# Delta rule and two mixers on one core: chunks of 64 on 64x64 array tiles, inverses by substitution on VectorE

## The chip, the cores and the metric

The kernel runs on one core of a Trainium2 chip. The metric is the device time of one execution in microseconds (us); lower is better. Engines are named as in the profile: PE (TensorE, matrix products), PEld (PE's weight loads, which run beside its products), DVE (VectorE), ACT (ScalarE), POOL (GpSimd), and SP, whose queue issues all DMAs here.

## What is computed

Four batches, eight heads, 768 tokens and 48 columns a head; everything is fp32. First the delta rule, a recurrence over the tokens, then a low-rank token mixer and a channel mixer (weights of 384x1536 and 1536x384):

```python
for t in range(S):                                  # attention, each head by itself
    y[t] = q[t] @ state
    state = state + beta[t] * outer(k_n[t], v[t] - k_n[t] @ state)
x  = y of the 8 heads side by side                  # (4, 768, 384)
u  = x + (x.T @ U @ V).T                            # rank 32
out = u + relu(u @ w_ch1) @ w_ch2
```

Here k_n is k divided by its norm.

## The kernel before

Tokens are taken in chunks of 128. In a chunk, with G[t, s] = k_t.k_s beta_s for s < t and S0 the state before it, the unknowns w solve (I + G) w = v - k S0; then y and the new state are products with w. So a chunk has a part that needs no state (`transposes`, `inverse`) and a part that does (`recur`).

`inverse` (line 319) runs for half of the heads (4) at a time. It makes the Gram products (`p_g`, L334, on 48 rows of the array, the two heads of a pair on the upper and the lower half of its rows), masks them into `bt`, `mt` and `qk` (L343), and builds the inverses of 32x32 blocks on PE: three rounds of `p_x` (L356) with two DVE operations each (L360, L361), then three levels of `p_m` and `p_x` (both through `per_head`, L250), each with a DVE transpose (L258), an expansion to block-diagonal form on POOL (`w_d`, L266), a mask (L370) and a subtraction (L375). A last level, `p_z` and `p_v`, makes 64x64 blocks. In all those products a 128x128 stationary matrix, mostly zeros, meets a moving one of 32 or 128 columns.

`recur` (L394) does `p_b` (L407), `rhs` on DVE, `p_c`, a copy `w` on ACT, `p_r`, a copy, `p_w` (these two with 64x64 stationary matrices, all in one corner of the array), the state (`p_s`, L438) and `p_y` (L454, L463). `mixer` (L475) is a batch's `p_tt`, then twice: `p_h`, `p_u`, 36 products `p_f` (L507) and 36 `p_o` (L521) of 384 columns. Each fp32 product is two matmul instructions with a weight load each in the profile; a transpose is one.

The order of the program is set by a heap of (time, step): each part's steps get a start and a distance. The mixer of a batch is spread over the next batch's chunks, and the last mixer has nothing beside it. The compiler's scheduler orders each engine's instructions from there. `load_weights` turns 27 slices of float64 weights into fp32, with seven DVE operations and one on POOL each, in the first 395 us.

Of the kernel before, what the change touches and what calls it, by code (L numbers as in the profile page):

```python
# [25 lines left out]
def kernel(  # L26
# [24 lines left out]
    NCH = S // C  # L51
# [20 lines left out]
    def ps_att(shape, name):  # L72
        return psum.tile(shape, FP32, name=name, tag="att", bufs=4)

    def ps_gram(shape, name):
        return psum.tile(shape, FP32, name=name, tag="gram", bufs=2)
# [5 lines left out]
    ident = const.tile([128, 128], FP32, name="ident")  # L82
    make_identity(nc, ident)

    def block_ones(t, m):
        nc.gpsimd.memset(t, 1.0)
        tv = t.rearrange("p (a i) -> p a i", i=m)
        n = C // m
        nc.gpsimd.affine_select(
            out=tv, in_=tv, pattern=[[-m, n], [0, m]], base=0,  # L90
            channel_multiplier=1, compare_op=ALU.is_ge, fill=0.0,
        )
        nc.gpsimd.affine_select(
            out=tv, in_=tv, pattern=[[m, n], [0, m]], base=m - 1,
            channel_multiplier=-1, compare_op=ALU.is_ge, fill=0.0,
        )

    def keep_upper(t):
        nc.gpsimd.affine_select(
            out=t, in_=t, pattern=[[1, C]], base=0,  # L100
            channel_multiplier=-1, compare_op=ALU.is_gt, fill=0.0,
        )

    def compact(name, t):
        c_t = const.tile([128, BK], FP32, name=name)
        nc.vector.tensor_reduce(
            out=c_t, in_=t.rearrange("p (a i) -> p i a", i=BK), axis=AX.X, op=ALU.add
        )
        return c_t

    bd = {m: const.tile([128, C], FP32, name=f"bd{m}") for m in (4, 8, 16, BK, HC)}
    for m, t in bd.items():
        block_ones(t, m)
    mask_u = const.tile([128, C], FP32, name="mask_u")
    nc.gpsimd.memset(mask_u, 1.0)
    keep_upper(mask_u)
    mask_b = const.tile([128, C], FP32, name="mask_b")
    nc.gpsimd.tensor_tensor(out=mask_b, in0=mask_u, in1=bd[BK], op=ALU.mult)
    mask_m = const.tile([128, C], FP32, name="mask_m")
    nc.gpsimd.tensor_tensor(out=mask_m, in0=mask_u, in1=mask_b, op=ALU.subtract)  # L120

    ident_c = compact("ident_c", ident)
    base_c = compact("base_c", bd[4])
    nc.vector.tensor_scalar_mul(base_c, base_c, -1.0)
    # lower off-diagonal blocks of m within the blocks of 2 m
    level_c = []
    for m in (4, 8, 16, BK):
        pool, tag = (conv, "power") if m < BK else (const, "mask_z")
        lev = pool.tile([128, C], FP32, name=f"lev{m}", tag=tag)
        nc.gpsimd.tensor_tensor(out=lev, in0=bd[2 * m], in1=bd[m], op=ALU.subtract)  # L130
        nc.gpsimd.affine_select(
            out=lev, in_=lev, pattern=[[-1, C]], base=0,
            channel_multiplier=1, compare_op=ALU.is_gt, fill=0.0,
        )
        if m < BK:
            level_c.append(compact(f"level{m}", lev))
    mask_z = lev

    def pads(name):
        ts = [const.tile([128, H, DP], FP32, name=f"{name}{i}") for i in range(2)]  # L140
        for t in ts:
            nc.vector.memset(t[:, :, D:DP], 0.0)
        return ts

    kpads, kbpads, qpads = pads("kpad"), pads("kbpad"), pads("qpad")
    # the states of two heads on the partitions, zero outside of a head's own columns
    states = [
        [const.tile([128, NP // 2, 2 * D], FP32, name=f"state{i}{g}") for g in range(2)]
        for i in range(2)
    ]  # L150
    for t in states[0] + states[1]:
        nc.vector.memset(t, 0.0)

    beta_sb = const.tile([BH, S], FP32, name="beta_sb")
    betas = const.tile([128, NCH, BH], FP32, name="betas")
    w1_sb = const.tile([128, KT, DFF], FP32, name="w1_sb")
    w2_sb = const.tile([128, FT, DM], FP32, name="w2_sb")
    u_sb = const.tile([128, NCH, R], FP32, name="u_sb")
    v_sb = const.tile([R, S], FP32, name="v_sb")

    def load_beta():
        nc.sync.dma_start(out=beta_sb, in_=beta.rearrange("b h s -> (b h) s"))
        p_bt = ps_att([128, NCH, BH], "p_bt")
        for c in range(NCH):
            nc.tensor.transpose(
                p_bt[:, c], beta_sb[:, c * C : (c + 1) * C], ident[0:BH, 0:BH]
            )
        nc.vector.tensor_copy(out=betas, in_=p_bt)
# [3 lines left out]
    def weight_slices():  # L172
        for t in range(KT):
            for f in range(0, DFF, WIDE):
                at = slice(f, f + WIDE)
                yield w1_sb[:, t, at], moe_w_ch1[t * 128 : (t + 1) * 128, at], None
        for f in range(FT):
            yield w2_sb[:, f], moe_w_ch2[f * 128 : (f + 1) * 128, :], None
        for s0 in range(0, S, WIDE):
            yield v_sb[:, s0 : s0 + WIDE], moe_V[:, s0 : s0 + WIDE], None  # L180
        yield u_sb.rearrange("p c r -> p (c r)"), moe_U, NCH

    def load_weights():
        """float64 to fp32. The upper word h has the sign, 11 bits of exponent and 20 of mantissa:
        with the exponent moved to fp32's bias they are an fp32 number, to which the lower word's
        part of the mantissa is added, which rounds. Below fp32's normal numbers, the exponent
        stops at 0."""
        for dst, src, groups in weight_slices():
# [10 lines left out]
            power_t = conv.tile([128, n], I32, name="power")  # L199
            upper_t = conv.tile([128, n], I32, name="upper")  # L200
# [31 lines left out]
    HH = H // 2  # L232
    PP = NP // 2
    raw, made, xs = {}, {}, {}

    def load(n):
        b, c = divmod(n, NCH)
        for name, src in (("k", k), ("q", q), ("v", v)):
            t = loads.tile([128, H, D], FP32, name=f"{name}_raw")
            nc.sync.dma_start(  # L240
                out=t, in_=src[b, :, c * C : (c + 1) * C, :].rearrange("h p d -> p h d")
            )
            raw[n, name] = t

    def over_heads(t):
        return t[:, None, :].to_broadcast([128, HH, BK])

    def per_head(ps, lhsT, rhs):
        for h in range(HH):
            nc.tensor.matmul(ps[:, h], lhsT[:, h], rhs[:, h], start=True, stop=True)  # L250

    def pair(t, j):
        return t[:, 2 * j : 2 * j + 2].rearrange("p h d -> p (h d)")

    def swapped(x):
        """Compact blocks, each transposed."""
        w_c = comp.tile([128, HH, BK], FP32, name="w_c")
        nc.vector.transpose(  # L258
            w_c.rearrange("p h i -> p (h i)"), x.rearrange("p h i -> p (h i)")
        )  # L260
        return w_c

    def expand(x, tag):
        """Compact blocks as a block-diagonal matrix for each head."""
        w_d = dense.tile([128, HH, C], FP32, name=tag)
# [10 lines left out]
    def transposes(n):  # L276
# [31 lines left out]
        for src, dst, copy in (  # L308
# [5 lines left out]
            for j in range(NP):  # L314
                nc.tensor.transpose(p_t[:, j], pair(src, j), ident)  # L315
# [279 lines left out]
```

## Time and profile before

| what | value |
|---|---|
| median of 3 runs | 1530.19 us (1515.23 to 1539.02) |
| profiled execution, first to last instruction (its span) | 1532.0 us |
| PE busy | 1485.9 us, 97% |
| DVE, POOL, ACT busy | 587.3, 363.7, 160.7 us |

The page gives the profiled execution no time beside its span; the span lies 1.8 us above the median, inside the runs' spread, so sums made against the span stand for the time. A matmul's duration in the profile reaches from its start to a modelled end and overlaps with the next one's, so the pace of a group is read from where it and the next group start.

### The profile page before, as it was taken

What the parts mean: (1) busy time and instruction counts of PE and PEld (TensorE: products, weight loads), DVE (VectorE), ACT (ScalarE), POOL (GpSimd) and SP (SyncE); (2) the same over time, 40 slices, a digit from 0 to 9 for tenths busy, and PEclk for the clock granted to TensorE, in tenths of its full rate; (3) what the DMA queues carried; (4) which work ended last, traced back from release to release, by engine and by line L of the source; (5) the groups of instructions that cost most, each with busy time, mean ns of one, the idle gap of its engine ahead of it and who ended that gap; (6) DMA issues with size and microseconds to landing.
All of it is one profiled execution on the core that took longest, in us unless ns stands there. A gap on an engine that the chain in (4) does not pass through costs nothing.

```text
span 1532.0 us, 20099 instructions
## 1 busy us (share of the span) xinstructions
PE 1485.9 (97%) x8238; PEld 1221.9 (80%) x8238; DVE 587.3 (38%) x1698; ACT 160.7 (10%) x386; POOL 363.7 (24%) x324
## 2 busy tenths in 40 slices
PE   6999899899999999999999999999999999999999
PEld 5999899899788887777877888787787888786555
DVE  5544665655524443343423442324423433321000
ACT  1000100100101111110111110101101000100110
POOL 3332242332222232132121231221231231120000
PEclk9855655655669998899677995799878997879889
DMA  3101111100100000000000010001000000000000
GB/s 90 42 22 37 47 36 42 47 26 22 26 1 16 22 21 6 16 21 12 16 11 6 22 27 0 16 1 26 22 1 6 11 11 6 1 1 16 0 16 16
DMA packets 82811, 30.10 MB, mean 20 GB/s; under 512 B 76480, under 2 KB 79552, under 8 KB 82720
## 3 DMA queue, kind: packets, MB, share of 16 engines
q1 hardware_dynamic: 82720, 28.81, 7.7%
q8 instruction: 66, 1.08, 0.3%
q14 instruction: 25, 0.20, 0.0%
HBM read 24.08 MB, written 4.72 MB: 19 GB/s over the span
## 4 chain that ended last, share of the span: by engine, by line
PE 92%; DVE 6%; issue 1%; POOL 1%; ACT 0%; DMA 0%; POOLq 0%; SPq 0%; DVEq 0%
PE p_f L507 16%; PE p_o L521 13%; PE p_m L250 12%; PE p_x L356 12%; PE p_x L250 11%; PE p_y L463 4%; PE p_g L334 3%; PE p_c L250 3%; PE p_w L250 3%; PE p_v L250 2%; PE p_r L250 2%; PE p_z L250 2%; PE p_s L438 2%; PE p_t L315 2%; PE p_y L454 2%; PE p_h L493 1%
## 5 line engine op out<-in xcount | busy, mean ns | idle before, releaser
L266 POOL TENSOR_TENSOR w_d<-w_c,bd 128x512 f32<-128x512 f32 x192 | 249.4, 1305 | 763.2 <-DVE w_c L258 750.5
L507 PE MATMUL p_f<-ut,w_sb 128*128 128x384 f32 x576 | 265.7, 604 | 2.8 <-ACT ut L501 2.8
L521 PE MATMUL p_o<-w_sb,h_f 128*128 128x384 f32 x576 | 207.9, 499 | 0.0
L250 PEld LDWEIGHTS p_m<-x_c,bt 128*128 128x128 f32 x1152 | 196.1, 256 | 14.0 <-issue 3.8
L250 PEld LDWEIGHTS p_x<-m_c,w_d 128*128 128x128 f32 x1152 | 192.3, 251 | 18.7 <-issue 9.9
L250 PE MATMUL p_m<-x_c,bt 128*128 128x32 f32 x1152 | 197.3, 329 | 0.7 <-DVE x_c L361 0.7
L250 PE MATMUL p_x<-m_c,w_d 128*128 128x32 f32 x1152 | 191.5, 324 | 0.0
L507 PEld LDWEIGHTS p_f<-ut,w_sb 128*128 128x128 f32 x576 | 123.2, 231 | 70.8 <-issue 30.4
L356 PEld LDWEIGHTS p_x<-x_c,bt 128*128 128x128 f32 x768 | 133.6, 260 | 20.6 <-issue 11.8
L521 PEld LDWEIGHTS p_o<-w_sb,h_f 128*128 128x128 f32 x576 | 103.5, 192 | 54.5 <-issue 1.2
L356 PE MATMUL p_x<-x_c,bt 128*128 128x32 f32 x768 | 135.4, 333 | 7.7 <-DVE x_c L361 7.7
L375 DVE TENSOR_TENSOR x_c<-x_c,p_x 128x128 f32<-128x128 f32 x144 | 41.5, 288 | 220.6 <-PE p_x L250 220.6
L360 DVE TENSOR_TENSOR x_c<-p_x,base_c 128x128 f32<-128x128 f32 x144 | 41.0, 290 | 214.7 <-PE p_x L356 214.7
L370 DVE TENSOR_TENSOR m_c<-p_m,level 128x128 f32<-128x128 f32 x144 | 42.0, 292 | 190.3 <-PE p_m L250 190.3
L266 POOL TENSOR_TENSOR w_d<-x_c,bd 128x512 f32<-128x512 f32 x48 | 61.0, 1278 | 93.9 <-DVE x_c L375 91.4
L515 ACT ACTIVATE h_f<-p_f 128x384 f32<-128x384 f32 x96 | 47.1, 491 | 342.4 <-PE p_f L507 342.4
L356 PEld LDWEIGHTS p_x<-ident_c,bt 128*128 128x128 f32 x384 | 58.6, 226 | 16.4 <-DVE bt L343 10.1
L356 PE MATMUL p_x<-ident_c,bt 128*128 128x32 f32 x384 | 63.1, 306 | 3.8 <-DVE bt L343 3.2
L334 PE MATMUL p_g<-kq,kbt 48*128 48x256 f32 x384 | 61.6, 434 | 4.5 <-DVE qk L343 3.3
L463 PE MATMUL p_y<-w,qk 128*128 128x48 f32 x384 | 65.0, 325 | 0.0
L531 DVE TENSOR_TENSOR o_sb<-p_o,x 128x384 f32<-128x384 f32 x24 | 13.3, 556 | 133.1 <-PE p_o L521 133.1
L250 PEld LDWEIGHTS p_z<-w_d,mt 128*128 128x128 f32 x384 | 57.1, 226 | 9.1 <-POOL w_d L266 5.3
(96 smaller groups left out, 1546.5 us busy)
## 6 DMA issues: line engine op xcount, KB each, us to landing
wide<-in_moe_w_ch_dram SPq DMA_DIRECT2D x24, 384.0 KB, 3.1
k_raw<-in_k_dram SPq DMA_DIRECT2D x24, 192.0 KB, 2.5
q_raw<-in_q_dram SPq DMA_DIRECT2D x24, 192.0 KB, 3.0
v_raw<-in_v_dram SPq DMA_DIRECT2D x24, 192.0 KB, 2.6
out_dram<-o_sb SPq DMA_DIRECT2D x24, 192.0 KB, 1.9
wide<-in_moe_V_dram SPq DMA_DIRECT2D x2, 96.0 KB, 2.0
wide<-in_moe_U_dram SPq DMA_DIRECT2D x1, 192.0 KB, 2.6
beta_sb<-in_beta_dram SPq DMA_DIRECT2D x1, 96.0 KB, 2.1
```

The source lines that it names most:

```text
L250: nc.tensor.matmul(ps[:, h], lhsT[:, h], rhs[:, h], start=True, stop=True)
L266: nc.gpsimd.tensor_tensor(out=w_d.rearrange("p h (a i) -> p h a i", i=BK), in0=x[:, :, None, :].to_broadcast([128, HH, NB, BK]), in1=bd[BK ...
L315: nc.tensor.transpose(p_t[:, j], pair(src, j), ident)
L334: nc.tensor.matmul(p_gs[par][:, i], kbt[lo : lo + D, j], kq[lo : lo + D, j], start=True, stop=True,)
L356: nc.tensor.matmul(p_x[:, h], bt[:, h], ident_c if it == 0 else x[:, h], start=True, stop=True)
L360: nc.vector.tensor_tensor(out=x, in0=p_x, in1=over_heads(base_c), op=ALU.mult)
L370: nc.vector.tensor_tensor(out=m_c, in0=p_m, in1=over_heads(mask), op=ALU.mult)
L375: nc.vector.tensor_tensor(out=x_new, in0=x, in1=p_x, op=ALU.subtract)
L463: nc.tensor.matmul(p_y[:, h], qk[:, h], w[:, h], start=(c == 0 and h == 0), stop=(h == HH - 1), skip_group_check=True,)
L507: nc.tensor.matmul(p_f, w1_sb[:, t, f * 128 : (f + 1) * 128], ut[:, t], start=(t == 0), stop=(t == KT - 1),)
L515: nc.scalar.activation(h_f, p_f, ACTF.Relu)
L521: nc.tensor.matmul(p_o, hs[f][:, c * C - g : (c + 1) * C - g], w2_sb[:, f], start=(f == 0), stop=(f == FT - 1),)
```

## The change

The chunk becomes 64 tokens (`L`), so there are 12 to a batch. A unit is half of a batch, 6 chunks of 8 heads; its work without state is done at once, and there are 8 units.

- The heads lie as 4 slots (pair j, parity par) times 2 halves g. Products of `grams`, `recur` (64x64 stationary matrices, 48 or 2x64 columns) and `below` (32x32) each use a quarter or less of the array; the order `QUADS` goes round its four quarters.
- The explicit inverse by doubling is gone, with its POOL expansions. A unit's 192 diagonal 32x32 blocks are brought to 96 partitions by row of blocks: `pg` is written to a DRAM scratch in pieces of 128 bytes (4 DMAs), read back as 96x1024 (1 DMA), inverted by 31 steps of two DVE operations each (`prod`, then a subtraction from `xt`), written to DRAM (1 DMA) and read back into `zt` and `zc` (6 DMAs). `below` makes the block under the diagonal with `p_x` and `p_v` (48 products each).
- `p_r` and `p_w` fall away; a chunk has five groups of 8 products, `p_b`, `p_y`, `p_c`, `p_s`, `p_y`.
- k, q and v come in 24 smaller DMAs a unit in place of 3 a chunk. PSUM has two tiles of two banks (`pair`) for `p_g`, `p_x`, `p_v`, `p_y`, `p_b`, `p_s`.
- The mixer's products stay; `o_sb` goes, `h_f` has 12 buffers in place of 14. The heap's times are new.

```diff
+QUADS = ((0, 0), (1, 1), (1, 0), (0, 1))
...
+    def grams(n):
...
+                    for par, g in QUADS:
+                        rows, cols = slice(DP * par, DP * par + D), slice(L * g, L * g + L)
+                        nc.tensor.matmul(
+                            p_g[cols, par, c, :, j],
+                            kq[rows, c0 + c, j, 0, cols],
+                            kq[rows, c0 + c, j, :, cols],
...
+    def blocks(n):
...
+        for i in range(4):
+            g, a = divmod(i, 2)
+            nc.sync.dma_start(
+                out=scr[CS * i : CS * i + CS].rearrange("q i j -> i q j"),
+                in_=pg[BK * i : BK * i + BK].rearrange("p r c j t -> p (r c j) t")[
+                    :, :, BK * a : BK * a + BK
+                ],
+            )
...
+        nc.sync.dma_start(out=gs, in_=scr)
+        yield
+        nc.vector.tensor_tensor(
+            out=gs, in0=gs, in1=cp[:, None, :].to_broadcast([NP, BK, BK]), op=ALU.mult
+        )
...
+        for j in range(BK - 1):
+            m, w = j + 1, BK - 1 - j
+            prod = step.tile([NP, m, w], FP32, name="prod", tag="prod", bufs=1)
+            nc.vector.tensor_tensor(
+                out=prod,
+                in0=gs[:, j : j + 1, j + 1 :].to_broadcast([NP, m, w]),
+                in1=xt[:, 0:m, j : j + 1].to_broadcast([NP, m, w]),
+                op=ALU.mult,
+            )
+            nc.vector.tensor_tensor(
+                out=xt[:, 0:m, j + 1 :], in0=xt[:, 0:m, j + 1 :], in1=prod, op=ALU.subtract
+            )
...
+        nc.sync.dma_start(out=scr2, in_=xt)
...
+        for i in range(4):
...
+            nc.sync.dma_start(
+                out=zt[BK * i : BK * i + BK].rearrange("p r c j t -> p (r c j) t")[
+                    :, :, BK * a : BK * a + BK
+                ],
+                in_=src,
+            )
+            if a == 0:
+                nc.sync.dma_start(out=zc[BK * g : BK * g + BK], in_=src)
...
+    def recur(b, c):
...
+        heads = [(j, par, g) for j in range(2) for par, g in QUADS]
...
+        p_c = ps_one([128, 4, D], "p_c")
+        for j, par, g in heads:
+            nc.tensor.matmul(
+                p_c[half(g), 2 * j + par],
+                zt[half(g), par, cu, j],
+                rhs[half(g), 2 * j + par],
...
+    FIRST, PERIOD = 95.0, 140.0
...
+        t0 = (-40.0, -18.0, 27.0, 50.0)[n] if n < 4 else FIRST + PERIOD * (b - 2) + 65.0 * (hf + 1)
+        at(t0, 0, load, n)
+        at(t0 + 3, 1, norms, n)
+        at(t0 + 4, 1, grams, n)
+        at(t0 + 14, 2.5, blocks, n)
+        at(t0 + 38, 1, below, n)
...
+            t0 = 3.5 * c + 4 if b == 0 else FIRST + PERIOD * (b - 1) + 11 * c
+            at(t0, 1, recur, b, c)
+        at(FIRST + PERIOD * b, PERIOD * 0.95 / MIX_STEPS, mixer, b)
+    at(-20.0, 4.0, load_weights)
```

How the instructions stand, at three places. First PE in the first chunk's inverse before (x_c and m_c are compact blocks, w_d the expanded ones, bt the Gram blocks; x4 is four heads):

```order
L250 MATMUL p_m<-x_c_277,bt_210 128x32 x4
L250 MATMUL p_m<-x_c_285,bt_225 128x32 x4
L250 MATMUL p_x<-m_c,w_d_290 128x32 x4
L250 MATMUL p_x<-m_c,w_d_307 128x32 x4
L250 MATMUL p_m<-x_c_321,bt_210 128x32 x4
L250 MATMUL p_m<-x_c_328,bt_225 128x32 x4
L250 MATMUL p_x<-m_c,w_d_332 128x32 x4
L250 MATMUL p_x<-m_c,w_d_343 128x32 x4
L250 MATMUL p_m<-x_c_357,bt_210 128x32 x4
L250 MATMUL p_m<-x_c_364,bt_225 128x32 x4
L250 MATMUL p_x<-m_c,w_d_368 128x32 x4
L250 MATMUL p_x<-m_c,w_d_381 128x32 x4
```

and now, from the second unit's last Gram products (x16) to the first chunk's state and output:

```order
L276 MATMUL p_g<-kq 64x2x64 x16
L364 MATMUL p_x<-zt_95,pg 32x32 x48
L379 MATMUL p_v<-xz,zn 32x32 x48
L441 MATMUL p_c<-vn,zt_95 64x48 x8
L455 MATMUL p_s<-z,kn_92 64x48 x8
L473 MATMUL p_y<-z,qk 64x48 x8
```

The three levels of doubling are gone from PE; 96 small products for a whole unit stand in their place, and behind them the recurrence.

Second, PE beside a mixer before, where `p_f` is the mixer's and all else the delta rule's:

```order
L507 MATMUL p_f<-ut,w_sb 128x384
L250 MATMUL p_x<-m_c,w_d_5286 128x32 x4
L463 MATMUL p_y<-w_5155,qk_4780 128x48 x4
L507 MATMUL p_f<-ut,w_sb 128x384 x2
L250 MATMUL p_x<-m_c,w_d_5308 128x32 x4
L250 MATMUL p_m<-x_c_5327,bt_5157 128x32 x4
L463 MATMUL p_y<-w_5177,qk_4800 128x48 x4
L250 MATMUL p_m<-x_c_5346,bt_5179 128x32 x4
L507 MATMUL p_f<-ut,w_sb 128x384 x3
L250 MATMUL p_x<-m_c,w_d_5350 128x32 x4
L250 MATMUL p_x<-m_c,w_d_5367 128x32 x4
L507 MATMUL p_f<-ut,w_sb 128x384 x3
```

and now, in the third mixer:

```order
L417 MATMUL p_b<-s,kq 64x48 x8
L429 MATMUL p_y<-s,kq 64x48 x8
L521 MATMUL p_f<-ut,w_sb 128x384
L441 MATMUL p_c<-rhs,zt_96 64x48 x8
L521 MATMUL p_f<-ut,w_sb 128x384
L455 MATMUL p_s<-z,kn_93 64x48 x8
L473 MATMUL p_y<-z,qk 64x48 x8
L521 MATMUL p_f<-ut,w_sb 128x384
L417 MATMUL p_b<-s,kq 64x48 x8
L429 MATMUL p_y<-s,kq 64x48 x8
L521 MATMUL p_f<-ut,w_sb 128x384
L441 MATMUL p_c<-rhs,zt_96 64x48 x8
```

A chunk's five groups of eight stand with a single mixer product between those that wait for each other.

Third, SP's queue at the start of the program before:

```order
L162 DMA beta_sb<-in_beta_dram 32x768
L240 DMA k_raw<-in_k_dram 128x8x48
L240 DMA q_raw<-in_q_dram 128x8x48
L240 DMA v_raw<-in_v_dram 128x8x48
L240 DMA k_raw<-in_k_dram 128x8x48
L240 DMA q_raw<-in_q_dram 128x8x48
L240 DMA v_raw<-in_v_dram 128x8x48
L196 DMA wide<-in_moe_w_ch_dram 128x768 x2
```

and now, for the first unit and the beginning of the second:

```order
L206 DMA vn<-in_v_dram 64x6x48 x8
L247 DMA cp<-cts 24x32 x4
L161 DMA wide<-in_moe_w_ch_dram 128x768
L206 DMA kn_93<-in_k_dram 64x6x48 x2
L303 DMA scr<-pg 32x24x32 x4
L206 DMA kn_93<-in_k_dram 64x6x48 x2
L310 DMA gs<-scr 96x1024
L206 DMA kn_93<-in_k_dram 64x6x48 x4
L206 DMA qn<-in_q_dram 64x6x48 x8
L206 DMA vn<-in_v_dram 64x6x48 x8
L161 DMA wide<-in_moe_w_ch_dram 128x768 x4
L336 DMA scr_542<-xt 96x1024
```

The loads that went straight through now share the queue with transfers that wait for other engines: scr for ACT's copies of pg, gs for scr's landing, scr_542 for the end of the substitution on DVE.

## Rows read from the trace of the kernel before

**Rows 1.** The page: span, then busy time, share and instructions by engine

```profile
span 1532.0 us, 20099 instructions
...
PE 1485.9 (97%) x8238; PEld 1221.9 (80%) x8238; DVE 587.3 (38%) x1698; ACT 160.7 (10%) x386; POOL 363.7 (24%) x324
```

**Rows 2.** The page: the chain that ended last, by line

```profile
PE p_f L507 16%; PE p_o L521 13%; PE p_m L250 12%; PE p_x L356 12%; PE p_x L250 11%; PE p_y L463 4%; PE p_g L334 3%; PE p_c L250 3%; PE p_w L250 3%; PE p_v L250 2%; PE p_r L250 2%; PE p_z L250 2%; PE p_s L438 2%; PE p_t L315 2%; PE p_y L454 2%; PE p_h L493 1%
```

**Rows 3.** Groups of instructions: line, engine, op, shapes, count | busy us, mean ns | idle before

```profile
L250 PE MATMUL p_m<-x_c,bt 128*128 128x32 f32 x1152 | 197.3, 329 | 0.7 <-DVE x_c L361 0.7
...
L250 PE MATMUL p_x<-m_c,w_d 128*128 128x32 f32 x1152 | 191.5, 324 | 0.0
```

**Rows 4.** Busy time by stretch: from:to, length, each engine, TensorE clock, DMA

```profile
61.00:66.00 5.00, 5.00 (x45) 4.40 (x46) 4.49 (x13) 1.57 (x5) 0.12 (x1) 1.00 0.66 152
304.00:314.00 10.00, 9.81 (x54) 9.47 (x54) 5.09 (x18) 0.31 (x1) 2.02 (x2) 0.50 0.03 11
1421.00:1447.00 26.00, 25.71 (x72) 14.94 (x73) 0.00 (x0) 5.64 (x12) 0.00 (x0) 0.89 0.00 1
```

**Rows 5.** PE in order of time, at 306 us: start us, length us, engine, what

```profile
306.00 1.09 PE L250 MATMUL p_r<-w,mt 64*64 64x48 f32 x8
307.02 1.91 PE L356 MATMUL p_x<-x_c,bt 128*128 128x32 f32 x8
308.86 1.09 PE L250 MATMUL p_w<-r,t_d 64*64 64x48 f32 x8
```

**Rows 6.** PE in order of time, at 62 us

```profile
61.96 1.13 PE L334 MATMUL p_g<-kq,kbt 48*128 48x256 f32 x8
63.02 1.09 PE L250 MATMUL p_c<-v_raw,t_d 128*128 128x48 f32 x8
64.05 0.66 PE L250 MATMUL p_r<-w,mt 64*64 64x48 f32 x8
64.64 1.08 PE L356 MATMUL p_x<-ident_c,bt 128*128 128x32 f32 x8
```

**Rows 7.** PE weight loads in order of time, at 64 and at 72 us

```profile
64.04 0.54 PEld L250 LDWEIGHTS p_r<-w,mt 64*64 64x64 f32 x8
...
71.80 0.93 PEld L250 LDWEIGHTS p_w<-r,t_d 64*64 64x64 f32 x8
```

**Rows 8.** PE in order of time: the last batch's mixer

```profile
1408.29 4.06 PE L481 MATMUL p_tt<-x,u_sb 128*32 128x384 f32 x12
...
1421.29 26.17 PE L507 MATMUL p_f<-ut,w_sb 128*128 128x384 f32 x72 [0.57 <-ACT ut L501]
...
1447.30 23.38 PE L521 MATMUL p_o<-w_sb,h_f 128*128 128x384 f32 x72
...
1505.05 23.38 PE L521 MATMUL p_o<-w_sb,h_f 128*128 128x384 f32 x72
```

**Rows 9.** SP's queue in order of time: the first load of k

```profile
1.25 0.41 SPq L240 DMA_DIRECT2D k_raw<-in_k_dram  x1
```

**Rows 10.** The page's DMA issues: line engine op, count, KB each, us to landing

```profile
k_raw<-in_k_dram SPq DMA_DIRECT2D x24, 192.0 KB, 2.5
```

**Rows 11.** PE in order of time: transposes at 9 us

```profile
9.04 1.06 PE L315 MATMUL p_t<-ident,qpad 128*128 128x128 f32 x4
```

**Rows 12.** DVE in order of time, two dependent operations at 29 us

```profile
28.90 0.29 DVE L360 TENSOR_TENSOR x_c<-p_x,base_c 128x128 f32<-128x128 f32 x1 [1.42 <-PE p_x L356]
29.11 0.48 DVE L361 TENSOR_TENSOR x_c<-x_c,ident_c 128x128 f32<-128x128 f32 x2
```

**Rows 13.** Groups of instructions on DVE and ACT, as rows 3

```profile
L360 DVE TENSOR_TENSOR x_c<-p_x,base_c 128x128 f32<-128x128 f32 x144 | 41.0, 290 | 214.7 <-PE p_x L356 214.7
...
L384 DVE TENSOR_TENSOR z<-p_z,lev 128x512 f32<-128x512 f32 x48 | 32.9, 686 | 31.4 <-PE p_z L250 31.4
...
L217 DVE TENSOR_SCALAR upper<-wide 128x384 int32<-128x384 int32 x24 | 12.7, 528 | 0.0
...
L421 ACT COPY w<-p_c 128x192 f32<-128x192 f32 x48 | 15.3, 319 | 177.6 <-PE p_c L250 168.2 <-issue 9.4
```

More of the change, by code (lines that the diff above doesn't have):

```diff
@@ L124 @@
[L124 to L136, printed above, removed]
@@ L155 @@
-    betas = const.tile([128, NCH, BH], FP32, name="betas")
+    upper = conv.tile([128, 128], FP32, name="upper", tag="power", bufs=1)
+    nc.gpsimd.memset(upper, 1.0)
+    nc.gpsimd.affine_select(
+        out=upper, in_=upper, pattern=[[1, 128]], base=0,
+        channel_multiplier=-1, compare_op=ALU.is_gt, fill=0.0,
+    )
+    mask_u = const.tile([128, L], FP32, name="mask_u")
+    for g in range(2):
+        at = slice(L * g, L * g + L)
+        nc.gpsimd.tensor_copy(out=mask_u[at], in_=upper[at, at])
@@ L229, in load_weights @@
             )
-    HH = H // 2
-    PP = NP // 2
-    raw, made, xs = {}, {}, {}
+    raw, made, xs, states = {}, {}, {}, {}
     def load(n):
[L237 to L265, printed above, removed]
-        nc.gpsimd.tensor_tensor(
-            out=w_d.rearrange("p h (a i) -> p h a i", i=BK),
-            in0=x[:, :, None, :].to_broadcast([128, HH, NB, BK]),
-            in1=bd[BK].rearrange("p (a i) -> p a i", i=BK)[:, None].to_broadcast(
-                [128, HH, NB, BK]
+        b, hf = divmod(n, 2)
@@ new lines, in load @@
+        vn = unit.tile([128, UC, 4, D], FP32, name="vn")
+        for t, src in ((kns[n % 2], k), (qn, q), (vn, v)):
+            for g in range(2):
+                for s in range(4):
+                    nc.sync.dma_start(
+                        out=t[L * g : L * g + L, :, s, 0:D],
+                        in_=src[b, 4 * g + s, hf * UC * L : (hf + 1) * UC * L, :].rearrange(
+                            "(c t) d -> t c d", t=L
+                        ),
+                    )
+        raw[n] = vn
@@ L334, in inverse, with below @@
+        made[n, "zc"] = zc
+    def below(n):
+        pg, zt, zc = made[n][1], zts[n % 2], made.pop((n, "zc"))
+        zn = single.tile([2 * BK, CS, BK], FP32, name="zn")
+        nc.vector.transpose(
+            zn.rearrange("p q t -> p (q t)"), zc.rearrange("p q t -> p (q t)")
+        )
+        p_x = ps_pair("p_x")
+        for e in range(CS):
+            r, c, j = e // (2 * UC), e // 2 % UC, e % 2
+            for g in range(2):
+                rows = slice(L * g + BK, L * g + L)
                 nc.tensor.matmul(
-                    p_gs[par][:, i],
@@ L391, in inverse @@
[L391 to L410 removed]
+        xz = single.tile([2 * BK, 2, 2 * UC * BK], FP32, name="xz", tag="zc")
@@ new lines, in below @@
+        nc.scalar.copy(xz, p_x[0 : 2 * BK, :, 0 : 2 * UC * BK])
+        yield
+        p_v = ps_pair("p_v")
+        for e in range(CS):
+            r, at = e // (2 * UC), slice(BK * (e % (2 * UC)), BK * (e % (2 * UC)) + BK)
+            for g in range(2):
+                rows = slice(BK * g, BK * g + BK)
+                nc.tensor.matmul(
+                    p_v[L * g : L * g + BK, r, at], zn[rows, e], xz[rows, r, at],
+                    start=True, stop=True,
+                )
+        for g in range(2):
+            rows = slice(L * g, L * g + BK)
+            nc.scalar.mul(
+                zt[rows].rearrange("p r c j t -> p r (c j) t")[:, :, :, BK:L],
+                p_v[rows, :, 0 : 2 * UC * BK].rearrange("p r (q t) -> p r q t", t=BK),
+                -1.0,
+            )
@@ L479, in mixer @@
         p_t = ps_mix([R, DM], "p_tt")
-        for c in range(NCH):
+        for c in range(NB):
             nc.tensor.matmul(
-                p_t, u_sb[:, c], x[:, c], start=(c == 0), stop=(c == NCH - 1)
+                p_t, u_sb[:, c], x[:, c], start=(c == 0), stop=(c == NB - 1)
             )
```

456 lines of the change are left out of this document (208 added, 248 removed).

## The prediction

> **What bounds the kernel now.** I read the page's shares first: PE is busy 97% of the span, no other engine over 38% [rows 1]. Then the chain that ended last, by line [rows 2]: `p_f` and `p_o`, the mixer, hold 29% of the span; `p_m` and the two `p_x`, the inverse by doubling, hold 35%. Then the groups: `p_m` and `p_x` have 1152 instructions each [rows 3] for products of 32 columns. Then what sets the pace of such a group. At a granted clock of 0.50, which is 1.2 GHz [rows 4], eight `p_x` start at 307.02 and the next group at 308.86, so one takes 0.23 us; eight `p_r`, with 64 stationary columns in place of 128, take 1.02 us, 0.128 each [rows 5]. At a clock of 1.00 (2.4 GHz) [rows 4] eight `p_r` take 0.59 us, 0.074 each, and eight `p_c` with 128 stationary columns 1.03, 0.129 each [rows 6]. Width of the stationary matrix sets the pace, not the few moving columns. The weight loads fill these groups: eight of 64 columns take 0.54 us at the higher clock and 0.93 at the lower, 0.067 and 0.116 each [rows 7]. So the reader is to see a kernel bound by PE, whose delta rule is bound by weight loads.
>
> **What products on quarters of the array cost.** The change takes `p_m`, both `p_x` of the doubling, `p_z`, `p_r` and `p_w` off PE and puts in small products. Counted from the order of the changed kernel, a matmul being two instructions: `p_b` 352, `p_y` 736, `p_c` 384, `p_s` 352, `p_g` 384, `p_x` and `p_v` 384 each, together 2976 matmuls or 5952 instructions. No row shows four quarters in turn. One quarter alone is `p_r`: 0.074 and 0.128 us. Two halves of the rows in turn is `p_g`: eight instructions of 256 columns take 1.06 us, while 72 `p_f` of 384 columns in 26.17 us [rows 8] make 0.363 each, 0.242 for 256 columns and 1.94 for eight. So the two halves run beside each other, as four steps plus some 0.1 to 0.2 us to fill. I take that for the new products: a group of 16 instructions is eight weight loads of 64 columns plus 0.2 us, 8 x 0.067 + 0.2 = 0.74 us at the higher clock and 8 x 0.116 + 0.2 = 1.13 at the lower, or 0.046 and 0.071 an instruction. The bounds: all four quarters beside each other, four loads plus 0.2, 0.029 and 0.042; nothing beside anything, 0.074 and 0.128. I take the middle because the order goes round quarters that share rows in two cases of four, and only the gain between row halves has a row. The 32x32 products are taken at the same price; they are a quarter of the columns, so this may be too much.
>
> On weight loads the Trainium skill (TensorE: Matmul & The Clock Gate, "What overlaps and what doesn't") says that they overlap with running products only when the row group differs. `p_g` agrees for two row groups; by this rule the sum is the middle one.
>
> **Up to the first mixer.** At the lower clock, since only small products run there, as at 304 us (at 62 us the clock was up with small products too; I take the dearer).
> - SP issues 32 DMAs ahead of the first unit's work; the first load of k took 0.41 us in the queue [rows 9] and 2.5 to land [rows 10]. At 0.45 each, 14.4 + 2.5 = 17; q has landed at 14.
> - 24 transposes at 1.06/4 [rows 11] are 6.4, 96 instructions of `p_g` 6.8, a copy 0.7: 28.
> - Through DRAM: four issues and a landing 4.3, reading back 2.9: 35. No row has pieces of 128 bytes; k's 192-byte pieces are the nearest.
> - The substitution: dependent operations on 128 elements start 0.21 us apart [rows 12]; from 128 to 512 elements the duration grows from 290 to 686 ns [rows 13], 1.03 ns an element, which leaves 0.08 a start. The 62 operations have 10,912 elements: 62 x 0.08 + 11.2 = 16 us; with full durations (0.158 each over the elements) 21. I take 18, with 1 for the scaling ahead. In the order, 3 weight slices of seven operations stand within it, at 0.528 [rows 13] 11 us. That makes 65.
> - To DRAM 2.9, back in six DMAs 5.2: 73. `below`: 2 x 96 instructions 13.6, three copies 2.5: 89.
> - Batch 0's recurrence: 57 groups of 16 at 1.13 are 64; in each of 12 steps PE also waits for the copy of z, 0.319 by ACT's `w` [rows 13], with hand-over an estimated 0.55: 7. DVE's two operations a step lie beside `p_y`. 71 us.
> - Between the steps stand the second unit's `below` and the third's transposes and Gram products, 16 + 15 = 31.
>
> The first mixer starts at 89 + 71 + 31 = 191. Bounds by the two other prices: 148 and 277.
>
> **The three mixers with the delta rule beside them.** A mixer by rows 8: two times 26.2 + 23.4 is 99.2, `p_tt` 4.1; `p_h` and `p_u`, from 1412.4 to 1421.3 and before the second `p_f`, 17 with waits for DVE, of which I take 13 for work: 116, three times 348. At 0.89 [rows 4] these rows hold some of the lower clock already. The delta rule of batches 1 to 3, less two grams made earlier: 2184 matmuls, 4368 instructions at 0.046, 201. 125 transposes at 0.2: 25. DVE, ACT and POOL have room: DVE, the busiest at 38% [rows 1], loses the masks and subtractions of the inverse and gains 8 x 18 us. Waits inside recurrence steps lie beside the one mixer product that the order puts between (0.36 us) and beside `p_y`; I leave 15 us for them and for 226 changes of array shape. Sum 589.
>
> On those changes the skill (TensorEngine Tiling (Array Packing), "Key Properties") has a rule against this kernel: changing the tiling mode drains PE. In rows 5 the eight `p_r` between products of full width cost 1.02 us against 0.93 us of weight loads, so a change costs at most about 0.05 us here, and 226 of them 11; the trace leaves little of the rule.
>
> **The last mixer** has nothing beside it, before and now: from 1408.3 to 1532.0, 124 us. In all 191 + 589 + 124 = 904; span and time differ by 2 us, so 905.
>
> **The rivals.**
> 1. *Four quarters at once.* For it: halves do overlap fully. Against it: `p_g` shows two only. 148 + (348 + 127 + 25 + 15) + 124 = 787. The tiling page's "Theoretical Speedup" promises a product of both dimensions, which would be this case.
> 2. *No overlap, since one quarter's weight load holds up the next.* For it: weight loads already bound `p_r`. Against it: `p_g`. 277 + (348 + 323 + 25 + 15) + 124 = 1112; with the lower clock in part of the mixers more.
> 3. *The units come late.* PE takes instructions in order, and a `p_x` that waits for zt holds the mixer behind it. A unit's way by the numbers above is 4.3 + 2.9 + 19 + 8.1 = 34 us plus what stands between on DVE and SP, where scr_542's issue waits for DVE with other loads behind it. If 24 us of it are uncovered for units 2 to 7, 145 more: 1050. Against it: a mixer of 116 us gives room for two units.
> 4. *Slower.* Each small product waits until the one ahead has left the array, at every turn to another quarter. 5856 of the small instructions are on the path (the second unit's 96 Gram instructions lie under the first unit's way through DRAM), 1488 of them before the first mixer; without them the sum is 904 - 201 - 106 = 597. At (1532 - 597)/5856 = 0.16 us each the gain is gone. `p_r` in rows 5, on one quarter, is below it at 0.128, and turns between row halves cost less, not more; the price is only reached if turning between quarters adds a wait.
>
> **How the numbers follow.** Forecast 0.48, rival 1 0.25, rival 2 0.12, rival 3 0.12, rival 4 0.03. The range goes from a little under rival 1 to rival 2: 740 to 1115; above it lie a rival 2 with a low clock and rival 4, below it cheaper 32x32 products together with rival 1. A measurement here tells about 2% from no change (the three runs spread over 1.6%). All but rival 4 are faster by more; a result within 2% would need a cost between: faster 0.96, same 0.01, slower 0.03.
>
> **What would show it.** In the profile of the changed kernel: eight matmuls `p_b` (16 instructions) in about 0.74 us between mixer products, 0.5 for rival 1, 1.2 for rival 2; the substitution's 62 operations within 16 to 21 us where nothing stands between; the first `p_h` near 190 us, the last `p_tt` near 780; PE busy over 90% between. Waits of `p_x` for zt of tens of us would show rival 3. A first mixer after 280 us, or `p_f` at 0.6 us each through the middle, would make the sum wrong.

## The result and the profile after

The changed kernel takes 915.8 us (median of 4 runs, 914.5 to 920.1) where the kernel before, on the same chip, takes 1534.6 (4 runs): a ratio of 0.601 (0.597 to 0.605). The ratio is of fast runs alone, so the slowest run of the kernel before (1571.6 us) is not in it. The forecast was 905. It is right as a number, but not for the reasons it gave: in its three mixers it was wrong by 80 to 86 us twice, in opposite directions.

The page of the changed kernel, with busy times, chain by engine and chain by line, to set against [rows 1, 2]:

```profile
span 913.9 us, 17342 instructions
...
PE 706.4 (77%) x7484; PEld 437.0 (48%) x7484; DVE 362.9 (40%) x930; ACT 178.6 (20%) x386; POOL 59.3 (6%) x66
...
PE 64%; DVE 22%; ACT 4%; DMA 3%; SPq 3%; issue 3%; POOL 1%; ACTq 0%; DVEq 0%
PE p_f L521 21%; PE p_o L535 18%; DVE xt L330 6%; DVE prod L324 5%; PE p_c L441 3%; PE p_h L507 3%; PE p_y L473 3%; PE p_t L264 2%; PE p_g L276 2%; PE p_s L455 2%; PE p_tt L495 2%; PE p_u L514 2%; PE p_y L429 2%; PE p_v L379 2%; PE p_x L364 2%
```

PE's work fell by 780 us, from 1485.9 to 706.4, but the span by 618 only. The idle time of PE rose from 46 to 207 us; and DVE, which stood nowhere among the first lines of the chain before, holds 22% of it: `prod` and `xt`, the substitution, 11%.

PE in order of time, in the first batch's recurrence and then near the end of the third mixer (granted clock 0.50 from 98 to 104 us, 1.00 from 764 to 771); the columns are as in [rows 5]:

```profile
101.26 0.68 PE L455 MATMUL p_s<-z,kn 64*64 64x48 f32 x16 [0.42 <-ACT z L449]
101.72 0.95 PE L473 MATMUL p_y<-z,qk 64*64 64x48 f32 x14
...
765.86 0.45 PE L417 MATMUL p_b<-s,kq 48*64 48x48 f32 x16
766.13 0.41 PE L429 MATMUL p_y<-s,kq 48*64 48x48 f32 x16
766.47 0.91 PE L535 MATMUL p_o<-w_sb,h_f 128*128 128x384 f32 x2
767.32 0.67 PE L441 MATMUL p_c<-rhs,zt 64*64 64x48 f32 x16
767.91 1.56 PE L535 MATMUL p_o<-w_sb,h_f 128*128 128x384 f32 x4
769.40 0.45 PE L455 MATMUL p_s<-z,kn 64*64 64x48 f32 x16
769.67 0.63 PE L473 MATMUL p_y<-z,qk 64*64 64x48 f32 x16
770.23 8.01 PE L535 MATMUL p_o<-w_sb,h_f 128*128 128x384 f32 x24
```

Read from start to start: 16 instructions `p_b` take 0.27 us, `p_y` from the state 0.34, `p_s` 0.27; `p_c` takes 0.59 and `p_y` from z 0.56. At the lower clock, at 101.26, `p_s` takes 0.46. The forecast had 0.74 at the higher clock and 1.13 at the lower. The code tells why two kinds stand there: `p_b`, `p_s` and the first `p_y` take their rows from one index and their columns from another, and so use all four quarters; `p_c` and the second `p_y` take both from `half(g)`, and so use two quarters only, those on the diagonal. They cost about twice as much. So the order `QUADS` goes round all four quarters in the Grams and in three of a chunk's five groups only; `p_x` and `p_v` of `below`, which don't use it, have two 32x32 blocks.

PE's waits over the whole span, the longest sums (us in all, times, longest):

```profile
PE p_x L364 <- DMA zt<-scr: 44.4, 6, 30.0
PE p_ct L242 <- DVE ct L229: 39.6, 6, 28.2
PE p_tt L495 <- POOL u_sb L192: 28.6, 1, 28.6
```

PE around the longest `p_x` wait, in order of time, then busy times by stretch (columns as in [rows 4]):

```profile
387.73 0.63 PE L473 MATMUL p_y<-z,qk 64*64 64x48 f32 x16
389.10 1.49 PE L495 MATMUL p_tt<-x,u_sb 128*32 128x384 f32 x2 [0.73 <-ACT x L482]
420.61 0.28 PE L364 MATMUL p_x<-zt,pg 32*32 32x32 f32 x2 [30.02 <-DMA zt<-scr]
422.20 2.77 PE L364 MATMUL p_x<-zt,pg 32*32 32x32 f32 x94 [1.31 <-DMA zt<-scr]
```

```profile
375.00:388.00 13.00, 10.68 (x312) 8.25 (x312) 4.06 (x12) 5.38 (x13) 0.24 (x1) 1.00 0.44 83
388.60:390.60 2.00, 1.49 (x2) 0.18 (x2) 0.80 (x1) 0.44 (x2) 0.00 (x0) 0.50 0.36 71
390.00:421.00 31.00, 0.87 (x3) 0.18 (x2) 21.99 (x63) 0.00 (x0) 0.95 (x1) 0.50 0.14 28
421.00:453.00 32.00, 25.92 (x375) 16.98 (x376) 8.04 (x13) 7.48 (x15) 2.12 (x1) 0.50 0.22 43
454.00:464.00 10.00, 9.92 (x184) 6.91 (x185) 2.72 (x8) 6.42 (x13) 0.23 (x1) 1.00 0.13 26
```

A `p_x` for the next batch's first unit stands in PE's order ahead of the rest of this batch's recurrence and its mixer. Its zt isn't there until DVE has done 22 us of substitution, and PE does nothing for 30 us. The granted clock is 1.00 up to 388 us, 0.50 in the wait, and still 0.50 for the 32 us behind it, in which PE is busy for 25.9 us; from 454 us it is 1.00 again. It had fallen by 388.6 us, before the wait began at 390.6, so the wait alone did not bring it down; what kept it down behind the wait is not shown.

The first unit and the second, on DVE in order of time (`prod` and `xt` are the substitution, L167 is a weight's conversion):

```profile
38.84 0.19 DVE L324 TENSOR_TENSOR prod<-gs,xt 96x31 f32<-96x31 f32 x1
...
57.69 0.34 DVE L324 TENSOR_TENSOR prod<-gs,xt 96x175 f32<-96x175 f32 x1
57.95 0.35 DVE L167 TENSOR_SCALAR power<-wide 128x384 int32<-128x384 int32 x1
...
66.92 0.21 DVE L330 TENSOR_TENSOR xt<-xt,prod 96x31 f32<-96x31 f32 x1
...
99.41 1.22 DVE L312 TENSOR_TENSOR gs<-gs,cp 96x1024 f32<-96x1024 f32 x1
```

and ACT's operation that stands between the two:

```profile
66.97 1.16 ACT L219 ACTIVATE ksq<-kn 128x1152 f32<-128x1152 f32 x1 [21.66 <-DVE prod L324]
```

The second unit's squares `ksq` are written into the buffer (tag `gs`) that the first unit's substitution reads, so they wait for its end at 67; norms, Grams and the way through DRAM follow, and the second substitution starts at 101 and ends at 142. The conversion of U stands behind it on DVE, which is PE's wait of 28.6 us at `p_tt`.

### The profile page after: what moved, and what is told of

Its sections match the earlier page's. It is cut to its first block, busy times and chain, and to the rows that moved or that the text cites. A ratio compares the mean times of both kernels' runs of the same rounds, so it can differ in the third digit from the quotient of the medians.

```text
span 913.9 us, 17342 instructions
## 1 busy us (share of the span) xinstructions
PE 706.4 (77%) x7484; PEld 437.0 (48%) x7484; DVE 362.9 (40%) x930; ACT 178.6 (20%) x386; POOL 59.3 (6%) x66
## 4 chain that ended last, share of the span: by engine, by line
PE 64%; DVE 22%; ACT 4%; DMA 3%; SPq 3%; issue 3%; POOL 1%; ACTq 0%; DVEq 0%
PE p_f L521 21%; PE p_o L535 18%; DVE xt L330 6%; DVE prod L324 5%; PE p_c L441 3%; PE p_h L507 3%; PE p_y L473 3%; PE p_t L264 2%; PE p_g L276 2%; PE p_s L455 2%; PE p_tt L495 2%; PE p_u L514 2%; PE p_y L429 2%; PE p_v L379 2%; PE p_x L364 2%
## 5 line engine op out<-in xcount | busy, mean ns | idle before, releaser
L521 PE MATMUL p_f<-ut,w_sb 128*128 128x384 f32 x576 | 223.2, 533 | 3.4 <-ACT ut L515 3.4
L330 DVE TENSOR_TENSOR xt<-xt,prod 96x31 f32<-96x31 f32 (+15 forms) x248 | 89.5, 361 | 7.0
L324 DVE TENSOR_TENSOR prod<-gs,xt 96x31 f32<-96x31 f32 (+15 forms) x248 | 84.9, 342 | 7.3
L364 PE MATMUL p_x<-zt,pg 32*32 32x32 f32 x768 | 19.4, 211 | 44.4 <-DMA zt<-scr 44.4
L495 PE MATMUL p_tt<-x,u_sb 128*32 128x384 f32 x48 | 23.3, 610 | 31.6 <-POOL u_sb L192 28.6
L264 PE MATMUL p_t<-ident,kn 128*128 128x128 f32 x96 | 30.8, 342 | 15.7 <-DMA kn<-in_k_dram 15.7
L482 ACT COPY x<-p_y 64x192 f32<-64x192 f32 x96 | 30.0, 313 | 52.1 <-PE p_y L473 51.5
L276 PE MATMUL p_g<-kq 48*64 48x128 f32 x768 | 35.6, 319 | 5.4 <-ACT kq L269 4.0
L441 PE MATMUL p_c<-rhs,zt 64*64 64x48 f32 x704 | 34.3, 246 | 6.8 <-DVE rhs L425 6.8
L441 PEld LDWEIGHTS p_c<-rhs,zt 64*64 64x64 f32 x704 | 29.5, 160 | 19.6 <-DVE rhs L425 18.0
L473 PE MATMUL p_y<-z,qk 64*64 64x48 f32 x768 | 36.6, 242 | 1.9 <-ACT z L449 1.9
L192 POOL TENSOR_TENSOR w_sb<-upper,power 128x384 f32<-128x384 f32 x24 | 24.7, 1028 | 158.9 <-DVE power L188 158.9
```

The costliest lines, as they stand in the source:

```text
L264: nc.tensor.transpose(p_t[:, j, i], t[:, c, 2 * j : 2 * j + 2].rearrange("p s d -> p (s d)"), ident,)
L276: nc.tensor.matmul(p_g[cols, par, c, :, j], kq[rows, c0 + c, j, 0, cols], kq[rows, c0 + c, j, :, cols], start=True, stop=True,)
L324: nc.vector.tensor_tensor(out=prod, in0=gs[:, j : j + 1, j + 1 :].to_broadcast([NP, m, w]), in1=xt[:, 0:m, j : j + 1].to_broadcast([NP, m, ...
L330: nc.vector.tensor_tensor(out=xt[:, 0:m, j + 1 :], in0=xt[:, 0:m, j + 1 :], in1=prod, op=ALU.subtract)
L364: nc.tensor.matmul(p_x[BK * g : BK * g + BK, r, BK * (e % (2 * UC)) : BK * (e % (2 * UC)) + BK], pg[rows, r, c, j, 0:BK], zt[rows, r, c, j ...
L441: nc.tensor.matmul(p_c[half(g), 2 * j + par], zt[half(g), par, cu, j], rhs[half(g), 2 * j + par], start=True, stop=True,)
```

## The experiments

Times are medians of the runs of that kernel; ratios are to the kernel before on the same chip (1536.7 to 1547.5 us there). Differences in us are to the 915.8 us of the changed kernel, beside which the kernel before took 1534.6.

**How the quarters overlap: e1.** The products are ordered by quarter, so that the same quarter is used several times in a row:

```diff
-            for c in range(2):
-                for j in range(2):
-                    for par, g in QUADS:
+            for par, g in QUADS:
+                for c in range(2):
+                    for j in range(2):
...
-        heads = [(j, par, g) for j in range(2) for par, g in QUADS]
+        heads = [(j, par, g) for par, g in QUADS for j in range(2)]
```

> The products of a group, and of the Gram stage, are put in order by quarter of the array, so that the two (in the Gram stage four) products of a quarter stand one behind the other. Theory A (products on different quarters run beside each other, and the queue of PE reaches over a few instructions): the pace of p_b and p_s (0.46 us for 16 at the lower clock, 0.24 to 0.26 at the higher) stays within 20%, time 905 to 930. Rival B (only neighbours in the queue overlap, so the turn order is what brings the pace): 0.7 to 0.9 us for 16 at the lower clock, p_g slower by half, some 20 to 40 us more, 935 to 955.

Measured 971.1 us (ratio 0.628, 0.623 to 0.634). The two stages part. The recurrence now has four instructions in a row on a quarter and keeps its pace (`p_s` from 113.02 to 113.48, 0.46 us, as after at 101 us); the Grams have eight in a row and lose it. The group of Gram products, busy in all, of the changed kernel and then of e1:

```profile
L276 PE MATMUL p_g<-kq 48*64 48x128 f32 x768 | 35.6, 319 | 5.4 <-ACT kq L269 4.0 <-DVE s L464 0.6 <-DVE rhs L425 0.4
```

```profile
L276 PE MATMUL p_g<-kq 48*64 48x128 f32 x768 | 88.7, 346 | 3.6 <-ACT kq L269 2.4 <-DVE xt L330 0.7 <-ACT x L482 0.4
```

One group of 32 in order of time, with transposes beside it, again of the changed kernel and then of e1:

```profile
21.38 1.98 PE L276 MATMUL p_g<-kq 48*64 48x128 f32 x32 [0.46 <-ACT kq L269]
23.30 0.47 PE L264 MATMUL p_t<-ident,kn 128*128 128x128 f32 x1
23.57 0.42 PE L264 MATMUL p_t<-ident,qn 128*128 128x128 f32 x1
23.78 0.42 PE L264 MATMUL p_t<-ident,kn 128*128 128x128 f32 x1
```

```profile
34.61 0.42 PE L264 MATMUL p_t<-ident,kn 128*128 128x128 f32 x1
34.82 0.42 PE L264 MATMUL p_t<-ident,qn 128*128 128x128 f32 x1
35.17 4.71 PE L276 MATMUL p_g<-kq 48*64 48x128 f32 x32
```

The traces record no change of clock before these groups (in e1 none before 172 us, so that a stretch like 112 to 115 is shown at 1.00 there), but the transposes beside both start 0.21 us apart; in the changed kernel that goes to 0.11 from 27 us on, when the clock is at 1.00. So I take both groups, and e1's `p_s`, to be at the lower clock. Then a group takes 1.92 us in the changed kernel, from its start to the next instruction's, and 4.71 in e1. The difference of 53 us in busy time is about the whole loss of 55. In e1 an instruction costs 4.71/32 = 0.147 us, no less than one quarter by itself in [rows 5] (0.128, with 48 columns): nothing overlaps, and that is why the time is above what either theory gave.

**Four in a row: e10.**

```diff
-                for j in range(2):
-                    for par, g in QUADS:
+                for par, g in QUADS:
+                    for j in range(2):
```

> The changed kernel with one loop of the Grams exchanged: four instructions in a row on a quarter of the array, where the changed kernel has two and e1 had eight. If what counts is how far ahead of a busy quarter the queue still starts others, and four instructions are within its reach (as the recurrence's runs of four in e1 were, p_s 16 in 0.46 us): p_g 32 in about 1.8 us at the low clock, as after, and the time 905 to 925. If any run longer than the changed kernel's costs overlap in the Grams, whose right sides are 128 columns wide and not 48: p_g 32 in 2.5 to 3.5 us and the time 930 to 955.

Measured 913.1 us (0.593, 0.586 to 0.600), in the first range. The same group of 32 in order of time:

```profile
21.42 2.05 PE L276 MATMUL p_g<-kq 48*64 48x128 f32 x32 [0.46 <-ACT kq L269]
23.40 0.47 PE L264 MATMUL p_t<-ident,kn 128*128 128x128 f32 x1
```

It takes 1.98 us, where after has 1.92: four in a row cost next to nothing with 128 columns either. Overlap holds at four and is gone at eight; why it ends is not shown.

**What the substitution costs: e2.** The 31 steps are left out; the blocks are scaled and moved, and not inverted.

```diff
-        for j in range(BK - 1):
+        for j in range(0):
```

> Left out: the 31 steps of the substitution (62 DVE operations a unit), so the inverses are wrong; the transfers through DRAM and all waits stay. Theory A (the start is bound by DVE, with 21 us of substitution a unit and the weights' conversion, and PE's later waits for zt end on DVE): first p_h from 207 to 160-170 us, PE's waits of p_x for zt from 44 to under 10, time 815 to 850. Rival C (it is the way through DRAM and SP's queue that is late): waits of p_x for zt stay over 30, first p_h over 185, time 880 to 900.

Measured 767.9 us, one run beside the kernel before: 148 us less, more than either theory gave. The first `p_h` starts at 149.7 us in place of 207.6, and 493 us lie from there to the last mixer's `p_tt`, 583 after. A stretch of this kernel:

```profile
300.00:400.00 100.00, 99.74 (x1233) 61.17 (x1232) 14.89 (x33) 26.49 (x57) 3.31 (x3) 1.00 0.21 45
```

So the substitution, eight times about 22 us of DVE's time (the groups `xt` and `prod`, 89.5 and 84.9 us), costs 58 us ahead of the first mixer and 90 in the three mixers, although DVE is busy 40% of the span. From 300 to 400 us PE without it is full, at a granted clock of 1.00.

**Whether the weights' conversion holds the start: e3.** Six of seven VectorE operations of a conversion are left out; the weights are other numbers.

> Left out: six of the seven DVE operations of a slice's conversion (the weights are wrong); loads and the POOL operation stay. Theory A: the second unit's substitution, which stands one to one with conversions from 101 to 141 us, takes 22 in place of 40, and p_tt no longer waits 29 us for u_sb; first p_h at 155 to 170, the rest as before, time 865 to 885. Rival C: the start is held by transfers and by PE's lower clock; first p_h over 190, time over 895.

Measured 894.0 us in one run, 22 less, just under rival C's bound. The first `p_h` starts at 190.2, as C had it and not A. The second substitution takes 32 us in place of 41, where A had 22. The wait for U falls from 28.6 to 7.3 us, but that of `p_x` for zt grows from 44.4 to 65.8: the second unit's chain is next.

**Where the late units stand: e4.** The rows under the diagonal (`below`) of units 3 to 7 are planned just ahead of their use, and not 38 units of plan after their load. No work changes.

```diff
-        at(t0 + 38, 1, below, n)
+        need = FIRST + PERIOD * (b - 1) + 66 * hf - 4
+        at(t0 + 38 if n < 3 else need, 1, below, n)
```

> The heap times of below (p_x, p_v) of the units 3 to 7 are set just ahead of the recurrence step that needs them, where they were 38 after the unit's start; nothing else. Theory A (PE takes instructions in order, and p_x of a unit that is late holds steps of the batch before and the mixer behind it): the waits of p_x for zt of 30 and 10 us at 420 and 615 go below 5 each, time 865 to 890. Rival C (the unit is late for whoever needs it): p_c or p_x waits as long at the new place, time 905 to 925.

Measured 837.1 us (0.541, 0.540 to 0.543), 79 less and below both ranges. PE's longest waits in this kernel:

```profile
PE p_ct L242 <- DVE ct L229: 37.6, 4, 28.3
PE p_tt L495 <- POOL u_sb L192: 28.6, 1, 28.6
```

From the first `p_h` to the last mixer's `p_tt`, first the changed kernel, with the wait for zt in that stretch, and then e4:

```profile
PE p_x L364 <- DMA zt<-scr: 43.1, 4, 30.0
207.60:790.20 582.60, 503.40 (x5471) 304.38 (x5471) 224.95 (x577) 125.20 (x276) 21.78 (x20) 0.86 0.19 41
```

```profile
207.70:710.40 502.70, 481.03 (x5472) 288.66 (x5472) 219.48 (x577) 124.89 (x276) 22.02 (x20) 0.95 0.22 48
```

No wait of `p_x` for zt is left; the first `p_h` stays at 207.7 and the last mixer's `p_tt` starts at 710.4 in place of 790.2. The 80 us between the two stretches are 58 of idle time of PE (79.2 against 21.7, where the waits for zt were 43.1) and 22 of busy time: the same instructions at a mean granted clock of 0.86 against 0.95.

**The second unit's buffer: e5.** The squares go into the tile `pg`, which is free then, and not into the buffer that the first substitution reads.

```diff
-        ksq = single.tile([128, UC, 4, D], FP32, name="ksq", tag="gs")
+        pg = unit.tile([128, 2, UC, 2, L], FP32, name="pg")
+        ksq = pg.rearrange("p r c j t -> p (r c j t)")[:, 0 : UC * 4 * D].rearrange(
+            "p (c s d) -> p c s d", s=4, d=D
+        )
```

> ksq, the squares for the norms, is written into the unit's pg tile (before pg is made) in place of the buffer that it shares with gs; nothing else. In the changed kernel the second unit's squares wait for the end of the first unit's substitution, 22 us, and PE waits 28 us for ct behind them. Theory D (this shared buffer puts the two first units one behind the other, and not DVE's load alone): p_ct's wait of 28 us goes, the second unit's substitution starts at 67 to 75 in place of 100, first p_h at 170 to 185, time 875 to 895. Rival A (DVE is the bound of the start: two substitutions and the conversions are the same work): first p_h at 200 to 208, time 905 to 920.

Measured 893.9 us (0.581, 0.577 to 0.585). The second substitution ends at 119 and not at 142, the first `p_h` starts at 185.3 and not at 207.6, and the whole gain of 22 us is that, as theory D had it. The three mixers are as long as before (582.3 us): waits for zt fall there from 43.1 to 24.8 us, and waits for converted weights (`w_sb`) of 16.8 us come in their place.

**A longer way through DRAM: e6.** A copy from DRAM to DRAM is put between writing and reading the blocks.

```diff
+        nc.sync.dma_start(out=scr3, in_=scr)
-        nc.sync.dma_start(out=gs, in_=scr)
+        nc.sync.dma_start(out=gs, in_=scr3)
```

> One DMA more on each unit's way: scr is copied to a second DRAM scratch before gs is read from that, about 3 us of transfer a unit. Theory A (units come late because of DVE's substitution and the order; the way through DRAM counts only where a unit is waited for): the two first units and the two waited for at 420 and 615, 4 x 3 = 12 us, time 922 to 932. Rival C (transfers and SP's queue set the pace of every unit): 8 x 3 and more, as SP's queue waits for each hop, time over 940. Rival E (all hidden): 914 to 918.

Measured 937.9 us (0.609, 0.605 to 0.613), 22 more, between the ranges of A and C. The first substitution starts 3.6 us later and the first `p_h` 8.2 (two units in a row). The waits for zt in the three mixers grow from 43.1 to 55.0 us, at two places, by 5 and 7. So a unit's way counts where it is waited for, as A had it, and in the mixers by more than its own length.

**Both edits: e7, and what holds it: e8, e9, e11.** E7 has the edits of e4 and e5.

> Both edits together: below of the units 3 to 7 just ahead of its use, and ksq in pg's tile. Theory A with D: the start's gain adds to that of the order, 837 less 20 to 35, 800 to 820. Rival: with the start shorter the third and fourth unit are the ones that are late, and p_x waits for zt again; 825 to 840.

Measured 836.2 us (0.544, 0.539 to 0.549): no gain over e4, though its first `p_h` starts at 186.2. That is in the rival's range, but not by its mechanism: no `p_x` waits for zt behind the first `p_h`. Between there and 300 us PE waits for weights (w_sb), and then for a copy of ACT in the rows of unit 3, which stand behind these products:

```profile
PE p_o L539 <- POOL w_sb L192: 11.3, 5, 4.6
PE p_v L383 <- ACT xz L376: 6.6, 1, 6.6
```

E8 is e7 with the conversion of e3:

> The kernel of e7 (rows of units 3 to 7 late, squares in the other buffer), with six of the seven VectorE operations that convert a slice of the mixer's weights left out (the weights are then wrong numbers; the sizes of all products stay). E7 started its first mixer 21.5 us earlier than e4 and ended no earlier. Theory W: the earlier start meets weights that are not converted yet (PE's waits for w_sb, 11.3 us, and the rows of unit 3 queued behind those products), so the start's gain comes back when the conversion is short: 805 to 820. Rival U: the units after the third are late whatever the weights do, because their chain of norms, Grams, substitution and transfers began later than the mixer needs: 827 to 838.

Measured 806.0 us (0.523, 0.522 to 0.525), in theory W's range. The three mixers take 504.2 us, where e7 has 521.5 and e4 502.7: with no weights to wait for, the start's gain comes back. Another 9 us come from the start itself (first `p_h` at 177.2). E9 computes everything and converts the weights earlier:

```diff
-    at(-20.0, 4.0, load_weights)
+    at(-20.0, 3.0, load_weights)
```

> The kernel of e7 with the slices of weights planned 3 units apart in the order of the work and not 4, nothing left out. Theory W: the waits for w_sb in the first mixer fall, at the price of more conversions among the first two substitutions (first p_h some us later than 186): 822 to 832. Rival U: no gain, 833 to 845, because the start gets later by as much as the waits fall.

Measured 818.6 us (0.530, 0.526 to 0.533), a little below W's range and the fastest kernel that leaves nothing out. The waits for `w_sb` are gone, the first `p_h` starts at 194.0, the last mixer's `p_tt` at 695.5. E11 plans the slices 2 apart:

> The kernel of e9 with the slices of weights planned 2 units apart and not 3. Theory W, taken further: the last waits for weights go, but the first substitutions get later: 815 to 830. Rival: the start pays more than the mixer gets, first p_h above 200: 830 to 845.

Measured 841.6 us (0.547, 0.542 to 0.551), as its rival said: the first `p_h` starts at 209.3, where e9 has 194.0. PE's wait at the first unit's `p_x` is about the same (27.1 us, e9 25.6); the second unit's `p_x` starts at 141.3 us in place of 130.9.

## Why the prediction was right, and where it was not

The forecast's three pieces, beside rival 1's and what the runs show (to the first `p_h`; from there to the last mixer's `p_tt`; the rest of the span):

| | forecast | rival 1 | after | e4 | e9 |
|---|---|---|---|---|---|
| to the first mixer | 191 | 148 | 207.6 | 207.7 | 194.0 |
| three mixers | 589 | 515 | 582.6 | 502.7 | 501.5 |
| last mixer | 124 | 124 | 123.7 | 123.7 | 123.1 |

- **What bounds the kernel before**: right. With the inverse and its wide weight loads off PE, PE's work fell by 780 us.
- **The price of a product on a quarter** failed. The forecast took two halves beside each other, 0.046 and 0.071 us an instruction; the four-quarter groups show 0.27/16 = 0.017 and 0.46/16 = 0.029, below even rival 1's 0.029 and 0.042, while `p_c` and the second `p_y`, on two quarters, show 0.035 to 0.037 at the higher clock. For these two the forecast's mechanism holds; that they differ from the rest stands in the code, and the forecast counted all as going round four quarters. The choice rested on `p_g` of before, which shows two row halves and can't show four quarters. As an estimate from the paces near 766 us, the recurrence of batches 1 to 3 costs 33 x 0.88 + 36 x 1.15 = 70 us, where the forecast's price makes 127 for these 171 groups. E4, without late units, runs the three mixers in 503 us, against 515 by rival 1 and 589 by the forecast: that is rival 1's mechanism. The count has a slip beside this: 2184 takes off one unit's Grams and not the two that the text says, 4 us.
- The Trainium skill's rule (TensorE: Matmul & The Clock Gate, "What overlaps and what doesn't") that weight loads overlap with running products only where the row group differs gave the middle price, too. Here it doesn't hold as a limit: `p_s` and `p_c` both have two row groups, and `p_s`, with two column groups to each, takes 0.27 us against 0.59; and `p_b`, whose neighbours share their rows at every second turn, takes 0.27 as well. What the Trainium skill states in TensorEngine Tiling (Array Packing), "Key Properties", that different tiles can load weights and multiply in parallel, agrees.
- **"I leave 15 us" for waits and changes of shape in the mixers** failed in the other direction. Late units and what follows them cost 80 us there (583 against 503). This is rival 3, which had the place and the mechanism right, PE's in-order `p_x` holding the mixer; its 145 us were too high. Its counter-argument, that a mixer of 116 us has room for two units, was true of the time and not of the order: e4 moves only where `below` stands, and the waits go. The changes of shape were also put too low, at 0.05 us each at most: two `p_o` between small groups take 0.85 us at 766.47, where 72 of them in [rows 8] make 0.325 each, so two changes cost about 0.2.
- **The start**: the way of the first unit was right to 2 us (end of the substitution 65, measured 67; end of `below` 89, measured 89.6). The substitution by itself took more: 48 of its 62 operations took 18.9 us, the whole an estimated 23 with the last 14 at the length of the first (4.2) where the forecast had 18 and at most 21; less conversion stood in it than was counted. What was left out is the second unit's own chain: the forecast put its products between the steps and not its wait for the first unit's buffer. E5 prices that buffer at 22 us. PE's wait for U belongs to the same chain: e3 takes most of it away and meets the `p_x` wait behind it. The start hides a balance of its own: `p_s` takes 0.46 us there where the forecast had 1.13, so its small products cost less than the forecast gave them, and the waits more.
- **Issue in SP's queue** at 0.45 us was too low: four loads of k took 2.60 us at 34 us, 0.65 each. What that costs in time was not tried.
- **Slower (rival 4) and no overlap (rival 2)** are excluded by the rows above, except for e1's Grams, which show what rival 2 would have been.

So the sum was right by luck: 86 us too much for the three mixers without late units (589 against e4's 503) stood against 80 us that the late units cost (583 against 503) and 17 us of the start (207.6 against 191). The rows asked for in the forecast did tell it: `p_b` in 0.27 us, under rival 1's 0.5, and waits of `p_x` of tens of us.

## What to carry to other kernels

Where small products go round the quarters of the array, count how many quarters a group can touch at once and price it by that, not by its count of instructions; keep the same quarter from coming up eight times in a row. Once PE's work is more than halved, the order of an in-order engine decides: put a product that waits for a long way through DVE and DRAM just ahead of its use, as e4 did for 79 us, and look for buffers that tie one unit's start to another's end. A faster start is worth only what the next supply, here the converted weights, can follow.

## What was not expected of the hardware

- Four quarters of 64 x 64 run beside each other in fp32: 0.27 to 0.34 us for 16 instructions, 3.5 to 4.4 times the pace of one quarter (8 in 0.59 us in [rows 6], between groups of full width).
- The overlap reaches over four instructions in a row on one quarter (e1's recurrence, e10) and not over eight (e1's Grams, 4.71 us against 1.92 for 32). Where between four and eight it ends was not tried.
- A stretch without work cost more than its length. Behind the wait of 30 us the granted clock was 0.50 for another 32 us, with PE busy for 26 of them; without such waits (e4) the mean clock of the three mixers was 0.95 and not 0.86.
